# Sparse attention and a gated feed-forward layer on one core: 120 score columns in place of 128, sums of exponentials in SBUF, and the first operations in another written order

## The chip, the cores and the metric

The kernel runs on one core of one Trainium2 chip. The metric is the device time of one execution in microseconds; the median of the runs is compared. The engines are TensorE (PE, with its weight loads shown as PEld), VectorE (DVE), ScalarE (ACT), GpSimd (POOL) and SyncE (SP), which issues nearly all DMAs.

## The reference

```python
# q, k, v: 4 batches, 8 heads, 768 positions, 64 dims, float32
k_sum = k.reshape(B, H, 24, 32, D).max(axis=3)       # summaries of blocks of 32
v_sum = v.reshape(B, H, 24, 32, D).mean(axis=3)
scores_l = scale * q @ k^T, kept where abs(i - j) < 16, else -1e9
scores_s = scale * q @ k_sum^T + log(32)
a = softmax over the 768 + 24 columns (1e-9 added to the sum)
x = a @ concat(v, v_sum)          # as 3072 tokens of 512
out = ((x @ w_a) * (x @ w_b)) @ w_out                # d_ff 1536
```

## The kernel before, in words

**Attention.** A batch's 768 queries are 6 tiles of 128, so there are 24 tiles. Ten chunks `u` of 2, 2, 2, 2, 2, 2, 3, 3, 3 and 3 tiles go through the feed-forward layer together. A tile is worked on as two halves `e` of 64 queries. One half needs 96 keys of the window and the 24 summaries, 120 columns; before, a block of scores has 128 columns, the last 8 of them padding. `kT` holds the transposed keys in periods of `PER` = 160 columns per tile: 96 of the window, 24 summaries, 8 zeros, 32 further keys. `scores` issues 32 matmuls per tile (4 head pairs, 2 heads, 2 halves), which use a quarter of the array each.

In the first two chunks (`u < 2`, `masked`) the mask is added by PE: `masks` multiplies an identity `identr` with `maskr`, 512 columns at a time, into the PSUM banks `o0` to `o3`, and the scores are added on top. ACT's exponentials (L746, eight per tile) read the bank and write `s` to SBUF; `accum_out` writes the sum of each into column 0 of the very block in the bank. DVE adds 1e-9 (L756), takes the reciprocal (L767), makes a diagonal of it (L774), and PE turns and normalizes the exponentials with this diagonal (L795). In the later chunks DVE adds the mask (L724), takes the negative maximum (L732), ACT takes the exponentials with sums in the small SBUF tile `nml`, POOL multiplies with the reciprocal (L782), and DVE transposes 32 rows by 256 columns at a time (L827). `products` (L843) multiplies with the values `vw`; ACT and DVE split the result into two fp32r parts `x` (L862, L866).

**Queries, values and means of the later chunks.** `qin` is filled by 16 loads per tile and DVE transposes it into `qT` (L1049). `prep_values` lets POOL add blocks of values in `S` (L624), scale the mean into `vm` (L649), and SP store its eight rows of heads to `S`; two loads bring them from there into `vw`. All of these transfers go through L342 on SP's queue.

**Weights.** The raw weight blocks (`raw`, L374) are converted: ACT scales (L409), DVE makes three steps (L417, L424, L430), ACT casts the high part (L462), POOL makes the low part (L467, L473). PSUM banks `c0`, `c1` serve the conversion and later the scores.

**Feed-forward.** An item is one of 12 blocks of 128 of d_ff for one chunk: matmuls `up` (L1097), ACT copy (L1129), DVE product (L1132), ACT cast (L1134), DVE subtraction (L1137), matmuls `down` (L1174).

**Order.** Every operation is recorded in `Work` with a rank and an estimated time, and has a number. `emit` issues first what the lists in `ORDER` name, one list per engine and in that order; after its end an engine takes the ready operation of lowest rank. An engine executes its instructions in the order of issue. `SPIN` (L1263) is a list of matmuls without use, which fill PE at the start and are ranked in `ORDER` too, with the numbers from 2701.

Of the kernel before, what the change touches and what calls it, by code (L numbers as in the profile page):

```python
# [15 lines left out]
ALU = mybir.AluOpType  # L16
AX = mybir.AxisListType
LOG32 = 3.4657359027997265
NEG = -1.0e9
# [12 lines left out]
        922-924 931 929 930 873 936-938 945 943 944 952 950 1015  # L32
    """,
    "ACT": """
        2 10 6 18 14 22 56 76 194 61-63 70 71 64 68 69 81 198 83 84 89 88 91 90 82 112 205 208
# [8 lines left out]
        932 934 939 941 946 948 878-882 885 953 886  # L44
    """,
    "DVE": """
        3 7 19 15 11 23 195 59 60 196 80 79 65 197 66 72 73 199 67 200 201 92 85 74 86 93 87 94
        209 210 213 211 214 215 223-225 126 227 125 228 155 156 138 131 139 132 140 133 117 147
# [6 lines left out]
        377 479 373 656 480 658 481 483-485 663 382 665 496 378 670 497 381 498 672 500-502 384  # L55
        383 677 732 511 513 733 514 512 734 679 735 745 684 736 746 520 747 737 686 738 527 739
        748 749 691 530 539 537 750 693 541 535 531 532 711 540 534 751 533 536 538 752 758 759
        713 718 702 760 708 761 771 762 763 772 764 773 765 720 774-776 912 832 777 778 914 698
        836 919 872 921 834 837 835 850 926 928 843 725 933 864 935 858 860 857 865 866 862 868
        863 867 940 942 861 859 874 947 875 949 876 877 883 1014 954  # L60
    """,
    "POOL": """
        36-38 29 26 32 35 95 97 101 99 105 103 203 206 217 110 108 204 220 207 218 231 221 232
        234 235 248 249 262 263 276 277 290 291 304 305 334 335 348 349 397 398 411 412 425 426
        439 365 453 372 454 456 440 457 470 471 473 474 487 488 490 491 504 505 507 508 529 521
        528 782-785 788 789 753 790-792 766 740 779 793 800-803 1405 851 844 806 1406 807 808
        1407 809-811 1409-1412 884
    """,
    "SP": """
# [14 lines left out]
    ("h1", 512), ("h1", 128), ("h1", 64), ("h1", 64), ("h1", 64), ("h1", 128), ("h1",  # L84
    128), ("h1", 128), ("h1", 128), ("h1", 128), ("h1", 256), ("h1", 256), ("h1", 256),
    ("h1", 128), ("h1", 256)
# [76 lines left out]
def attention_moe(  # L163
# [10 lines left out]
    nc = tc.nc  # L174
# [47 lines left out]
    PER = 160  # L222
# [5 lines left out]
    for c in range(NP):  # L228
        nc.gpsimd.memset(kper[:, c, :, WIN + NS : WIN + 32], 0.0)
# [5 lines left out]
    for i in range(3):  # L235
        for e in range(2):
            es = slice(e * QT, (e + 1) * QT)

            for c0, n, w in ((0, 96, 0),) if e == 0 else ((0, 32, 0), (64, 64, 32)):
# [12 lines left out]
            nc.gpsimd.memset(mask[es, i, k0 : k0 + NS], LOG32)  # L252
            nc.gpsimd.memset(mask[es, i, k0 + NS : k0 + 32], NEG)
# [3 lines left out]
    sbuf = sb([P, 2, NP, P], "s")  # L257
    pbuf = sb([P, 2, NP, P], "pt")
# [276 lines left out]
    def first_keys():  # L535
        n = P // BLK
        for i in range(S // P):
# [10 lines left out]
            def put(bk=bk, c0=c0):  # L548
# [3 lines left out]
                    out=kT[:, :, c0 + P : c0 + PER + 16], in_=tr[:, :, WIN - 16 :]  # L552
# [16 lines left out]
    def prep_keys(b):  # L569
# [3 lines left out]
        for c in range(NP):  # L573
# [5 lines left out]
            for takes, o, i in (  # L579
                (0.7, kper[:, c, :, :WIN], groups[:, :, :WIN]),  # L580
                (0.26, kper[:, c, :, P:], groups[:, :, WIN:]),
# [9 lines left out]
            for takes, o, i in (  # L591
                (0.65, half[:, :, :6], kper[:, c, :, :WIN].rearrange(x16, x=16)),
                (0.26, half[:, :, 6:], kper[:, c, :, P:].rearrange(x16, x=16)),
# [65 lines left out]
    def load_values(b, t, vw, keys, rank):  # L659
# [3 lines left out]
        for i, (e, r0, lo, hi) in enumerate((  # L663
            (0, skip, row - 16 + skip, row + 80),
            (1, 0, row + 48, row + 80),
            (1, 64, row + 80, end),
# [6 lines left out]
    def scores(u, t, qT, qk, s, sk, banks, diag=None, lead=None):  # L673
# [7 lines left out]
        def masks():  # L681
            for h in range(2):
                for part in range(2):
                    nc.tensor.matmul(
                        bank[banks[h]].rearrange("p (c x) -> p c x", x=P), identr,
# [614 lines left out]
```

## Time and profile before

| | |
|---|---|
| median of 3 runs | 668.29 us (667.89 to 670.66) |
| profiled execution | 667.98 us |
| its span in the profile | 666.2 us |
| mean granted PE clock | 0.999 |
| PE busy | 652.4 us, 98% of the span |
| DVE, ACT, POOL busy | 419.3, 257.4, 190.6 us |

The span is what the profiler records between the first and the last instruction; the execution's own time is 1.78 us longer. The rows quoted below give a start or a group, then its length in microseconds, the engine, the line of the code, and what is written from what, without the numbers of the buffers. A bracket at the end of a row is the idle time just before it and what ended it.

### The profile page before, as it was taken

What the parts mean: (1) busy time and instruction counts of PE and PEld (TensorE: products, weight loads), DVE (VectorE), ACT (ScalarE), POOL (GpSimd) and SP (SyncE); (2) the same over time, 40 slices, a digit from 0 to 9 for tenths busy, and PEclk for the clock granted to TensorE, in tenths of its full rate; (3) what the DMA queues carried; (4) which work ended last, traced back from release to release, by engine and by line L of the source; (5) the groups of instructions that cost most, each with busy time, mean ns of one, the idle gap of its engine ahead of it and who ended that gap; (6) DMA issues with size and microseconds to landing.
All of it is one profiled execution on the core that took longest, in us unless ns stands there. A gap on an engine that the chain in (4) does not pass through costs nothing.

```text
span 666.2 us, 14017 instructions
## 1 busy us (share of the span) xinstructions
PE 652.4 (98%) x5442; PEld 610.7 (92%) x5442; DVE 419.3 (63%) x900; ACT 257.4 (39%) x791; POOL 190.6 (29%) x255
## 2 busy tenths in 40 slices
PE   8899999999999999999999999999999999999996
PEld 6689999999899999999999999999999999999996
DVE  3999999996677777567677755686662531122222
ACT  4996675523444432234334413333331411121111
POOL 6588989755344432011111100101110100000000
PEclk9999999999999999999999999999999999999999
DMA  9999747365343244412122331232000200010001
GB/s 219 270 272 274 262 116 176 64 139 125 94 87 94 69 94 98 78 32 71 30 41 50 77 58 32 41 86 41 17 10 1 70 1 0 1 48 1 0 1 48
DMA packets 156619, 54.78 MB, mean 82 GB/s; under 512 B 134008, under 2 KB 149624, under 8 KB 156552
## 3 DMA queue, kind: packets, MB, share of 16 engines
q1 hardware_dynamic: 156408, 53.75, 33.8%
q8 instruction: 42, 0.69, 0.5%
q14 instruction: 25, 0.20, 0.1%
q10 hardware_dynamic: 144, 0.13, 0.1%
HBM read 47.12 MB, written 6.29 MB: 80 GB/s over the span
## 4 chain that ended last, share of the span: by engine, by line
PE 74%; DVE 9%; SPq 7%; DMA 6%; issue 2%; ACT 2%; POOL 1%; DVEq 0%; POOLq 0%
PE h L1097 44%; PE o L1174 23%; SPq L342 6%; DMA raw<-in_moe_w_b_dram 3%; PE o L843 3%; PE c L697 2%; DMA raw<-in_moe_w_out_dram 2%; DVE c L424 1%; SPq L374 1%; DVE S L827 1%; DVE S L417 1%; DVE h L1132 1%; DVE S L430 1%; DVE space L430 1%; DVE pt L827 1%
## 5 line engine op out<-in xcount | busy, mean ns | idle before, releaser
L1097 PE MATMUL h<-x,w 128*128 128x256 f32 (+1 forms) x2488 | 396.0, 295 | 0.0
L1097 PEld LDWEIGHTS h<-x,w 128*128 128x128 f32 x2488 | 356.2, 191 | 4.7 <-issue 0.2
L1097 PE MATMUL h<-late,w 128*128 128x256 f32 (+1 forms) x380 | 114.1, 300 | 0.0
L1174 PE MATMUL o<-w,gh 128*128 128x512 f32 x426 | 107.2, 383 | 0.0
L827 DVE STREAM_TRANSPOSE pt<-s 32x256 f32<-32x256 f32 x228 | 99.4, 436 | 11.5 <-POOL s L782 5.7
L782 POOL TENSOR_TENSOR s<-s,nml 128x512 f32<-128x512 f32 x40 | 41.6, 1040 | 211.7 <-DVE nml L767 210.2
L1160 DVE TENSOR_TENSOR h<-h,g 128x384 f32<-128x384 f32 x47 | 26.6, 566 | 112.1 <-PE h L1097 109.9
L1174 PEld LDWEIGHTS o<-w,gh 128*128 128x128 f32 x426 | 76.6, 189 | 9.6 <-issue 1.5
L1162 ACT CAST gh<-h 128x384 fp32r<-128x384 f32 x47 | 22.5, 479 | 143.0 <-DVE h L1160 142.5
L746 ACT ACTIVATE s<-s,nml 128x128 f32<-128x128 f32 x160 | 62.3, 391 | 38.1 <-DVE nml L732 38.1
L1097 PEld LDWEIGHTS h<-late,w 128*128 128x128 f32 x380 | 72.3, 190 | 1.1
L1129 ACT COPY g<-h 128x256 f32<-128x256 f32 x72 | 26.7, 370 | 101.5 <-PE h L1097 101.2
L1174 PE MATMUL o<-w,gl 128*128 128x512 f32 x213 | 60.0, 381 | 0.0
L1174 PE MATMUL o<-w,x 128*128 128x512 f32 x225 | 56.2, 382 | 0.0
L1132 DVE TENSOR_TENSOR h<-h,g 128x256 f32<-128x256 f32 x72 | 30.7, 426 | 29.4 <-ACT g L1129 28.3
L624 POOL TENSOR_TENSOR S<-S 96x256 f32<-96x256 f32 (+3 forms) x58 | 33.1, 572 | 54.5 <-DMA S<-in_v_dram 51.9
L1174 PEld LDWEIGHTS o<-w,gl 128*128 128x128 f32 x213 | 39.8, 189 | 6.4 <-DVE gl L1137 0.6
L1174 PEld LDWEIGHTS o<-w,x 128*128 128x128 f32 x225 | 40.1, 190 | 5.5 <-issue 0.5
L724 DVE SCALAR_TENSOR_TENSOR s<-c,mask 128x512 f32<-128x512 f32 x40 | 27.2, 684 | 19.6 <-PE c L697 19.6
L1157 ACT COPY g<-h 128x384 f32<-128x384 f32 x48 | 23.0, 479 | 41.0 <-PE h L1097 40.9
L1165 DVE TENSOR_TENSOR gl<-h,gh 128x384 fp32r<-128x384 f32 x47 | 26.1, 555 | 17.9 <-ACT gh L1162 17.5
L467 POOL TENSOR_TENSOR space<-space,w 128x1024 f32<-128x1024 f32 (+1 forms) x14 | 26.7, 1914 | 12.0 <-ACT w L462 11.6
(130 smaller groups left out, 654.8 us busy)
## 6 DMA issues: line engine op xcount, KB each, us to landing
raw<-in_moe_w_a_dram SPq DMA_DIRECT2D x12, 512.0 KB
raw<-in_moe_w_b_dram SPq DMA_DIRECT2D x12, 512.0 KB
raw<-in_moe_w_out_dram SPq DMA_DIRECT2D x12, 512.0 KB
out_dram<-S SPq DMA_DIRECT2D x23, 256.0 KB
S<-in_v_dram SPq DMA_DIRECT2D x24, 192.0 KB
kin<-in_k_dram SPq DMA_DIRECT2D x38, 100.0 KB
vw<-in_v_dram SPq DMA_DIRECT2D x18, 192.0 KB
qin<-in_q_dram SPq DMA_DIRECT2D x192, 16.0 KB
```

Of the source, the lines that this page charges most:

```text
L342: lambda: nc.sync.dma_start(out=out, in_=in_), rate=rate,
L467: lambda ms=ms, f8=f8: nc.gpsimd.tensor_tensor(out=f8, in0=f8, in1=parted(0)[:, ms].bitcast(F32), op=ALU.subtract),
L624: lambda: nc.gpsimd.tensor_tensor(out=out, in0=i0, in1=i1, op=ALU.add),
L724: lambda h=h: nc.vector.scalar_tensor_tensor(out=s[h], in0=bank[banks[h]].rearrange("p (c x) -> p c x", x=P), scalar=0.125, in1=mask[:, ki ...
L746: lambda h=h, c=c, sums=sums: nc.scalar.activation(s[h][:, c, :], x[h][:, c, :], AF.Exp, bias=m[:, 0, h, c : c + 1], scale=1.0, accum_out= ...
L782: lambda h=h, r=r: nc.gpsimd.tensor_tensor(out=s[h], in0=s[h], in1=r[:, :, None].broadcast_to([P, NP, P]), op=ALU.mult,),
L827: lambda js=js, qs=qs, rs=rs: nc.vector.transpose(out=pv[js, rs, qs], in_=sv[qs, rs, js]),
L1097: nc.tensor.matmul(ps, w[:, c, part, :], inputs_of(u, xpart)[:, :, c].rearrange("p g (a b) -> p g b a", a=2), start=(i == 0), stop=(i == n ...
L1129: act(CHAIN, 0.38, [hk], [gk], lambda: nc.scalar.copy(out=g, in_=pa))
L1132: lambda: nc.vector.tensor_tensor(out=pa, in0=pb, in1=g, op=ALU.mult),
L1160: lambda: nc.vector.tensor_tensor(out=pb, in0=pb, in1=g, op=ALU.mult),
L1174: nc.tensor.matmul(bank[ok[j]], (gh if first else gl)[:, j * P : (j + 1) * P], w[:, :, part, :].rearrange("p (z a) n -> p z n a", a=2), st ...
```

## The change

The block of scores has `KN` = 120 columns, and `PER` is 152. All operations on scores, mask and exponentials take 120 (or 4 x 120 = 480) columns; the matmuls that turn them, and the products, contract over 120 rows. The memsets of the padding in `kT` and in the mask go; one memset of the padding of `s` comes. In the first two chunks the exponentials' sums go to `nml` in SBUF, and the addition of 1e-9 reads them there. The lists in `ORDER` are written anew and go further than before on DVE, ACT, POOL, SP and PE; `SPIN` has 16 matmuls of other widths in place of 15. The lines of the code shift by two to four.

```diff
-    PER = 160
+    PER = WIN + NS + 32
+    KN = WIN + NS
...
-    for c in range(NP):
-        nc.gpsimd.memset(kper[:, c, :, WIN + NS : WIN + 32], 0.0)
...
-            nc.gpsimd.memset(mask[es, i, k0 + NS : k0 + 32], NEG)
...
+    nc.gpsimd.memset(sbuf[:, :, :, KN:], 0.0)
...
-                        bank[banks[h]].rearrange("p (c x) -> p c x", x=P), identr,
-                        maskr[part][:, kind, None, :].broadcast_to([P, NP, P]),
+                        bank[banks[h]].rearrange("p (c x) -> p c x", x=P)[:, :, :KN], identr,
+                        maskr[part][:, kind, None, :KN].broadcast_to([P, NP, KN]),
...
-                            bank[banks[h]][es, c * P : (c + 1) * P], qT[hs, c, es],
-                            kT[hs, c, c0 : c0 + P],
+                            bank[banks[h]][es, c * P : c * P + KN], qT[hs, c, es],
+                            kT[hs, c, c0 : c0 + KN],
...
-            sums = x[h][:, :, 0] if masked else l
+            sums, r = l, x[h][:, :, 0] if masked else l
...
-                        out=r, in0=r, scalar1=1e-9, scalar2=None, op0=ALU.add
+                        out=r, in0=l, scalar1=1e-9, scalar2=None, op0=ALU.add
...
-                        bank[banks[h]][:, c * P : (c + 1) * P], s[h][:, c, :], d[:, h, c, :],
+                        bank[banks[h]][:KN, c * P : (c + 1) * P], s[h][:, c, :KN], d[:, h, c, :],
...
-                            ps[h * D : (h + 1) * D, c, es], vw[e][:, 2 * c + h, :],
-                            d[:, h, c, es], start=True, stop=True, tile_position=(0, h * D),
+                            ps[h * D : (h + 1) * D, c, es], vw[e][:KN, 2 * c + h, :],
+                            d[:KN, h, c, es], start=True, stop=True, tile_position=(0, h * D),
```

```diff
 SP, the first numbers of its list in ORDER
-        0 8 4 16 12 20 39 40 186 42 44 41 43 187 46 45 189 190 53 192 54 193 49 48 52 47 50 51
+        12 0 4 8 39 16 20 40 186 187 42 41 44 43 45 189 53 46 190 54 192 193 47 49 48 50-52 237
```

SP, the first loads of the program (`space` holds keys, queries and values in pieces, `raw` a weight block). Before:

```order
L342 DMA space_183<-in_k_dram 128x8x64 x3
L342 DMA space_184<-in_k_dram 128x8x64
L342 DMA space_183<-in_k_dram 128x8x64
L342 DMA space_184<-in_k_dram 128x8x64
L342 DMA space_184<-in_q_dram 128x8x64 x2
L374 DMA raw_208<-in_moe_w_a_dram 128x4x256
L342 DMA space_185<-in_v_dram 128x4x128 x4
L374 DMA raw_208<-in_moe_w_b_dram 128x4x256
```

and now:

```order
L344 DMA space_174<-in_k_dram 128x8x64 x4
L344 DMA space_175<-in_q_dram 128x8x64
L344 DMA space_175<-in_k_dram 128x8x64 x2
L344 DMA space_175<-in_q_dram 128x8x64
L376 DMA raw_199<-in_moe_w_a_dram 128x4x256
L376 DMA raw_199<-in_moe_w_b_dram 128x4x256
L344 DMA space_176<-in_v_dram 128x4x128 x4
```

One block of queries now stands ahead of the last two blocks of keys, and the second weight block ahead of the four blocks of values.

SP, the end of the `qin` loads of the tile whose scores run at 175.71 us in the profile, and the transfers of the value means around them. Before:

```order
L342 DMA qin<-in_q_dram 32x8x32 x2
L342 DMA S_181<-in_v_dram 96x512
L342 DMA out_dram<-S_182 128x512
L342 DMA S_182<-vm 24x64 x3
L342 DMA qin<-in_q_dram 32x8x32
L342 DMA S_182<-vm 24x64
L342 DMA qin<-in_q_dram 32x8x32
L342 DMA vw_165<-S_182 24x512
```

and now:

```order
L344 DMA qin<-in_q_dram 32x8x32 x4
L344 DMA S_173<-vm 24x64
L344 DMA qin<-in_q_dram 32x8x32
L344 DMA S_173<-vm 24x64
L344 DMA qin<-in_q_dram 32x8x32
L344 DMA S_173<-vm 24x64 x2
L344 DMA vw_156<-in_v_dram 80x8x64
L344 DMA S_172<-in_v_dram 96x512
L344 DMA vw_157<-in_v_dram 32x8x64
L344 DMA vw_156<-S_173 24x512
```

Two of the four stores of means that stood ahead of the last `qin` load stand behind it now, and the loads of the means into `vw` follow a little later.

PE, the matmuls from just ahead of these scores to the products that follow (`c_77`, `c_78` are the banks of the scores, `o_71` and `o_72` those of the feed-forward output). Before:

```order
L1174 MATMUL o_71<-w_969,x 128x512 x2
L1174 MATMUL o_72<-w_969,x 128x512 x2
L697 MATMUL c_77<-kT,qT 64x128 x2
L697 MATMUL c_78<-kT,qT 64x128 x2
...
L1174 MATMUL o_71<-w_969,x 128x512
L1174 MATMUL o_72<-w_969,x 128x512
L1174 MATMUL o_71<-w_1164,gh 128x512 x2
L1174 MATMUL o_72<-w_1164,gh 128x512 x2
L843 MATMUL o_74<-pt,vw_165 64x64 x2
```

and now:

```order
L1178 MATMUL o_71<-w_976,x 128x512
L1178 MATMUL o_72<-w_976,x 128x512
L699 MATMUL c_77<-kT,qT 64x120 x2
L699 MATMUL c_78<-kT,qT 64x120 x2
...
L1178 MATMUL o_71<-w_1146,gh 128x512 x2
L1178 MATMUL o_72<-w_1146,gh 128x512 x2
L1178 MATMUL o_71<-w_1146,gl 128x512
L1178 MATMUL o_72<-w_1146,gl 128x512
L847 MATMUL o_74<-pt,vw_156 64x64 x2
```

Two `down` matmuls moved from behind the scores to ahead of them, and two others from behind the products to ahead of them.

More of the change, by code (lines that the diff above doesn't have):

```diff
@@ L25 @@
     "PE": """
[6 rows of a table removed]
-        922-924 931 929 930 873 936-938 945 943 944 952 950 1015
+        2701 2702 13 2703 1 2704 5 2705 2706 55 9 2707 17 2708 2709 21 57 75 77 58 78 2710-2712
+        96 98 2713 100 2714 143 102 104 111 113 121 141 106 123 151 124 153 154 2715 2716 115
+        145 171 173 542 180 175 178 549 547 182 548 554-556 563 570 561 562 568 575 577 569 584
[5 rows of a table added]
     """,
     "ACT": """
-        2 10 6 18 14 22 56 76 194 61-63 70 71 64 68 69 81 198 83 84 89 88 91 90 82 112 205 208
[8 rows of a table removed]
-        932 934 939 941 946 948 878-882 885 953 886
[7 rows of a table added]
@@ L45 @@
+        499 671 489 676 678 503 506 522 683 523-526 516 517 685 515 518 519 690 692 710 712 701
+        717 719 707 911 696 913 918 920 845 848 846 838 839 925 840 841 927 723 842 847 849 932
+        934 939 941 946 948 881 887 953 885 955 878 879 886 888 889 880 882 960 962 870 967
     """,
     "DVE": """
-        3 7 19 15 11 23 195 59 60 196 80 79 65 197 66 72 73 199 67 200 201 92 85 74 86 93 87 94
-        209 210 213 211 214 215 223-225 126 227 125 228 155 156 138 131 139 132 140 133 117 147
[6 rows of a table removed]
@@ L55 @@
[L55 to L60, printed above, removed]
+        3 15 7 11 19 23 195 196 60 59 80 199 197 200 79 92-94 201 65 66 72 67 85 73 74 86 209 87
@@ L61 @@
+        210 211 213-215 126 125 223 224 155 156 138 225 139 131 227 132 140 133 117 228 147 229
[3 rows of a table added]
+        595 357 355 358 356 389-391 393 600 394 602 395 403 404 607 405 407 609 408 417 409 418
[7 rows of a table added]
+        866-868 860 858 859 861 876 874 877 875 947 1014 949 954 725 956 890 1049 883 898 899
+        903 895 904 897 902 961 963 871 896 905 901 900
     """,
     "POOL": """
-        36-38 29 26 32 35 95 97 101 99 105 103 203 206 217 110 108 204 220 207 218 231 221 232
-        234 235 248 249 262 263 276 277 290 291 304 305 334 335 348 349 397 398 411 412 425 426
@@ L65 @@
-        439 365 453 372 454 456 440 457 470 471 473 474 487 488 490 491 504 505 507 508 529 521
-        528 782-785 788 789 753 790-792 766 740 779 793 800-803 1405 851 844 806 1406 807 808
-        1407 809-811 1409-1412 884
+        36-38 29 26 32 35 97 95 101 99 103 105 206 203 108 110 207 204 220 217 218 231 221 232
+        234 235 248 249 262 263 276 277 290 291 304 305 334 335 348 349 397 398 411 412 372 425
+        365 426 439 440 453 454 456 457 470 471 473 474 487 488 490 491 529 504 505 507 528 521
@@ L68 @@
+        508 782-785 788 789 753 790 740 791 792 766 779 793 800-803 1405 844 1406 851 806 1407
+        807-811 1409-1412 1414 891 884 1415-1417 1419 1420
     """,
     "SP": """
[8 rows of a table removed]
+        12 0 4 8 39 16 20 40 186 187 42 41 44 43 45 189 53 46 190 54 192 193 47 49 48 50-52 237
[8 rows of a table added]
     """,
@@ L83 @@
 SPIN = [
-    ("h1", 512), ("h1", 128), ("h1", 64), ("h1", 64), ("h1", 64), ("h1", 128), ("h1",
-    128), ("h1", 128), ("h1", 128), ("h1", 128), ("h1", 256), ("h1", 256), ("h1", 256),
-    ("h1", 128), ("h1", 256)
+    ("h1", 512), ("h1", 128), ("h1", 64), ("h1", 64), ("h1", 256), ("h1", 256), ("h1",
+    64), ("h1", 128), ("h1", 128), ("h1", 256), ("h1", 256), ("h1", 256), ("h1", 256),
+    ("h1", 256), ("h1", 256), ("h1", 256)
 ]
@@ L237, in attention_moe @@
             es = slice(e * QT, (e + 1) * QT)
-            for c0, n, w in ((0, 96, 0),) if e == 0 else ((0, 32, 0), (64, 64, 32)):
+            for c0, n, w in ((0, 96, 0),) if e == 0 else ((0, 32, 0), (32 + NS, 64, 32)):
                 sl = mask[es, i, c0 : c0 + n]
@@ L551, in put @@
                 nc.scalar.copy(
-                    out=kT[:, :, c0 + P : c0 + PER + 16], in_=tr[:, :, WIN - 16 :]
+                    out=kT[:, :, c0 + KN : c0 + PER + 16], in_=tr[:, :, WIN - 16 :]
                 )
@@ L580, in prep_keys @@
                 (0.7, kper[:, c, :, :WIN], groups[:, :, :WIN]),
-                (0.26, kper[:, c, :, P:], groups[:, :, WIN:]),
+                (0.26, kper[:, c, :, KN:], groups[:, :, WIN:]),
                 (0.15, kT[:, c, KC - 32 :], kw[:, S:]),
@@ L592, in prep_keys @@
                 (0.65, half[:, :, :6], kper[:, c, :, :WIN].rearrange(x16, x=16)),
-                (0.26, half[:, :, 6:], kper[:, c, :, P:].rearrange(x16, x=16)),
+                (0.26, half[:, :, 6:], kper[:, c, :, KN:].rearrange(x16, x=16)),
                 (0.1, ks[:, c, NS - 1, None], kT[:, c, KC - 32 : KC - 16]),
@@ L665, in load_values @@
             (1, 0, row + 48, row + 80),
-            (1, 64, row + 80, end),
+            (1, 32 + NS, row + 80, end),
         )):
@@ L715, in scores @@
             lead[3]()
-        x = [bank[n].rearrange("p (c x) -> p c x", x=P) for n in banks] if masked else s
+        y = [bank[n].rearrange("p (c x) -> p c x", x=P)[:, :, :KN] for n in banks]
+        s = [t[:, :, :KN] for t in s]
+        x = y if masked else s
         xk = banks if masked else sk
@@ L724, in scores @@
                     lambda h=h: nc.vector.scalar_tensor_tensor(
-                        out=s[h], in0=bank[banks[h]].rearrange("p (c x) -> p c x", x=P),
-                        scalar=0.125, in1=mask[:, kind, None, :].broadcast_to([P, NP, P]),
+                        out=s[h], in0=y[h],
+                        scalar=0.125, in1=mask[:, kind, None, :KN].broadcast_to([P, NP, KN]),
                         op0=ALU.mult, op1=ALU.add,
@@ L751, in scores @@
             lk = [f"{mk}l{h}{c}" for c in range(NP)]
-            r = sums
             if masked:
@@ L755, in scores @@
                     rank, 0.15, [xk[h]], lk,
[L756 to L757 removed]
+                    lambda l=l, r=r: nc.vector.tensor_scalar(
+                        out=r, in0=l, scalar1=1e-9, scalar2=None, op0=ALU.add
                     ),
@@ L782, in scores @@
                     lambda h=h, r=r: nc.gpsimd.tensor_tensor(
-                        out=s[h], in0=s[h], in1=r[:, :, None].broadcast_to([P, NP, P]),
+                        out=s[h], in0=s[h], in1=r[:, :, None].broadcast_to([P, NP, KN]),
                         op=ALU.mult,
@@ L807, in transposes @@
                     lambda h=h: nc.scalar.copy(
-                        out=d[:, h], in_=bank[banks[h]].rearrange("p (c x) -> p c x", x=P)
+                        out=d[:KN, h],
+                        in_=bank[banks[h]].rearrange("p (c x) -> p c x", x=P)[:KN],
                     ),
@@ L991, in first_attention @@
         for e, r0 in ((0, WIN), (1, 32)):
-            rows = slice(r0, r0 + 32)
+            rows = slice(r0, r0 + NS)
             act(
```

1 line of the change is left out of this document (removed), and 57 rows, old and new, of the table ORDER.

## The prediction

> **What bounds the kernel now.** I read the page's head first, then a table of windows by stage, then TensorE's waits, and only then the chain around the two places where TensorE stands still.
>
> ```profile
> span 666.2 us, 14017 instructions
> PE 652.4 (98%) x5442; PEld 610.7 (92%) x5442; DVE 419.3 (63%) x900; ACT 257.4 (39%) x791; POOL 190.6 (29%) x255
> ```
>
> TensorE (PE) works 652.4 of 666.2 us, so two things alone can shorten the span: fewer microseconds of matmul, or part of the 13.8 us in which PE is idle. The windows say where these lie (the columns after the length are PE, PEld, DVE, ACT, POOL, then the granted clock, which is full everywhere).
>
> ```profile
> 0.00:20.00 20.00, 16.14 (x132) 11.76 (x132) 9.32 (x16) 10.00 (x33) 12.85 (x64) 1.00 1.08 236
> 20.00:40.00 20.00, 17.02 (x209) 14.07 (x209) 18.35 (x39) 19.11 (x64) 11.79 (x12) 1.00 1.03 265
> 40.00:60.00 20.00, 20.00 (x203) 19.02 (x202) 19.99 (x40) 16.81 (x34) 17.77 (x10) 1.00 1.13 288
> 80.00:145.00 65.00, 65.00 (x553) 61.12 (x552) 62.31 (x131) 37.32 (x92) 52.19 (x37) 1.00 0.54 127
> 170.00:180.00 10.00, 8.52 (x106) 7.25 (x105) 5.64 (x14) 5.28 (x22) 5.70 (x10) 1.00 0.30 78
> 180.00:640.00 460.00, 460.00 (x3725) 436.06 (x3724) 259.95 (x572) 143.96 (x487) 59.70 (x93) 1.00 0.20 45
> 640.00:666.20 26.20, 20.72 (x116) 19.27 (x114) 5.67 (x11) 4.37 (x10) 0.00 (x0) 0.97 0.09 31
> ```
>
> Idle PE: 3.86 and 2.98 us in the first 40, 1.48 between 170 and 180, 5.48 at the tail, none elsewhere. In the first 40 us PE is not the bound (its work there is partly filler); what counts is when the feed-forward part starts. From then on PE is a solid row: the end is the start of that row, plus its matmuls, plus the one stall, plus the tail, which the change leaves as it is.
>
> ```profile
> 39.70 2.92 PE L1097 MATMUL h<-x,w 128*128 128x256 f32 x24
> PE c L697 <- DVE qT L1049: 1.5, 1, 1.5
> ```
>
> So the row starts at 39.70, and the stall is one wait of scores for the transposed queries. The profiled execution took 667.98 us (1.78 around the span); the median of the runs shown is 668.29, 0.05% more, so I add up against 667.98. A difference under 0.5%, 3.3 us, is about what a measurement of this kernel cannot tell from none.
>
> **Term 1: the scores lose 8 of 128 columns.** In chunks 2 to 9 there are 640 score matmuls, 32 for each of 20 tiles.
>
> ```profile
> L697 PE MATMUL c<-kT,qT 64*64 64x128 f32 x640 | 22.3, 275 | 1.5 <-DVE qT L1049 1.5
> L843 PE MATMUL o<-pt,vw 128*64 128x64 f32 x608 | 22.2, 225 | 0.0
> 175.71 1.10 PE c L697 x32
> 178.31 1.08 PE o L843 x32
> 180.02 5.36 PE h L1097 x48
> 372.86 3.90 PE h L1097 x24
> ```
>
> The first two rows are groups by shape; the others are pieces of the chain. 256 columns of the feed-forward matmul take 5.36/48 = 0.112 us, 384 columns 3.90/24 = 0.1625: 0.40 ns per column. The scores run four at a time, one per quarter of the array; eight fours in 1.10 us are seven steps and one duration of 0.275, 0.118 a step, close to the 0.112 of a 256-column pass. I read a four as 128 f32 columns gone over twice. Then 8 columns are worth 16 x 0.40 = 6.4 ns a four, 0.051 us a tile, 1.0 us over 20 tiles. Bounds: 0 if weights or issue pace the fours, and for this speaks that the products (L843), with half the columns, take 1.08 us for 32; 1.10/16 x 20 = 1.4 if all of the time is columns. I take **-1.0**, because with the products the weights have 128 rows and the single matmul is 225 ns against 275, so it is the columns that the longer one shows.
>
> The Trainium skill, TensorE: Matmul & The Clock Gate, section "Back-to-back issue gap", says that in a stream of weight loads and matmuls the spacing is set by both and gives about 81 ns for 128 columns. By that rule the loads could hide the columns and this term would be 0, the third rival below; the product row agrees with it, the score row does not decide.
>
> The 16 mask matmuls go from 512 to 480 columns, all before the row starts at 39.70, where PE has idle time: 0. The matmuls that turn the normalized scores and the products contract over 120 rows instead of 128, with the same columns: 0, between -0.1 and 0.1 (the score matmul with 64 rows and the product with 128 take the same 1.1 us for 32).
>
> **Other engines' shorter operations, after 40 us.** The mask addition, the maximum (0.68 us each on DVE), the exponentials and POOL's multiplication shrink by up to 1/16. From 180 to 640 DVE works 260 of 460 us, and PE never waits: 0. If anything were later there, the feed-forward items ahead of each attention step cover it; without that cover the chain of a tile would be some 0.04 us shorter at the addition and at the maximum (0.68/16), 20 x 0.08 = 1.6 us over the tiles, a gain. From 40 to 145 DVE is full, but PE has no idle there either, so its few shortened operations can only add slack. Eight memsets go and one comes, on POOL at the start, where it works 12.85 of 20 us: 0.
>
> **Term 2: the stall at 174 us.** SP issues the 16 `qin` loads of a tile; the last lands at 174.76 and DVE's transpose and the scores follow.
>
> ```profile
> 169.25 2.30 SPq L342 DMA_DIRECT2D S<-vm  x3
> 171.59 0.52 SPq L342 DMA_DIRECT2D qin<-in_q_dram  x1
> 172.16 0.72 SPq L342 DMA_DIRECT2D S<-vm  x1
> 172.92 0.51 SPq L342 DMA_DIRECT2D qin<-in_q_dram  x1
> 172.92 1.84 DMA qin<-in_q_dram
> 174.94 0.71 DVE L1049 STREAM_TRANSPOSE qT<-qin 128x512 f32<-128x512 f32 x1 [1.74 <-DMA qin<-in_q_dram]
> 175.71 1.10 PE L697 MATMUL c<-kT,qT 64*64 64x128 f32 x32 [1.48 <-DVE qT L1049]
> 173.97 0.75 SPq L342 DMA_DIRECT2D vw<-S  x1
> 175.33 0.73 SPq L342 DMA_DIRECT2D vw<-S  x1
> ```
>
> Before, four stores of value means (`S<-vm`, 0.72 to 0.77 us each) stand between or just ahead of the last loads; in the changed order two do, and the last load stands eight places earlier on SP. Two stores fewer bring it 1.5 us forward; the places passed (0.45 to 0.75 us each) more still, unless a store waits for POOL. From the issue to the scores it takes 175.71 - 172.92 = 2.79 us, so queries ready at 174.2 or earlier. PE was ready at 174.23 and now has two down matmuls (0.43 us) ahead of the scores. The wait goes: -1.48. What is late next are the mean rows `vw<-S`: the two loads now follow the stores closely, and the second issue, at 175.33 before, would land at about 176.5 if all of SP moves 1 us forward and a load takes the 1.84 us of the one above; the products would reach PE at about 176.55. A new wait lies between 0 and 0.5. The whole term lies between -1.48 and 0 (the wait kept, or turned into one at the products); I take **-1.4**.
>
> **Term 3: the start.** Two chunks' exponentials sum into column 0 of the PSUM bank that the next one reads; now they sum into SBUF.
>
> ```profile
> 9.24 0.66 PE L492 MATMUL o<-ident,space 128*128 128x128 f32 x4 [0.28 <-DMA space<-in_k_dram]
> 10.52 0.63 PE L492 MATMUL c<-ident,space 128*128 128x128 f32 x4 [0.17 <-DMA space<-in_k_dram]
> 17.77 0.37 ACT L746 ACTIVATE s<-o,nml 128x128 f32<-128x128 f32 x1
> 18.09 0.37 ACT L746 ACTIVATE s<-o,nml 128x128 f32<-128x128 f32 x1
> 18.55 0.37 ACT L746 ACTIVATE s<-o,nml 128x128 f32<-128x128 f32 x1
> 157.34 0.39 ACT L746 ACTIVATE s<-s,nml 128x128 f32<-128x128 f32 x1
> 157.72 0.39 ACT L746 ACTIVATE s<-s,nml 128x128 f32<-128x128 f32 x1
> L732 DVE TENSOR_REDUCE nml<-o 128x4 f32<-128x512 f32 x8 | 5.2, 681 | 0.1
> DVE space L417 <- ACT c L409: 3.6, 2, 3.0
> 15.50:40.00 24.50, 20.75 (x250) 16.21 (x249) 22.69 (x46) 22.12 (x78) 14.22 (x15) 1.00 1.06 274
> ```
>
> The PSUM sums start 0.32 or 0.46 us after one another (0.40 on the mean of two), those with SBUF sums 0.385. The new ones read PSUM and sum into SBUF, which no row shows; between 0.32 and 0.385 is likely, so 32 exponentials give ACT 0.5 to 2.6 us. But DVE decides: from 15.5 to 40 it works 22.69 of 24.50 us, and the same operations stand ahead of the first `x` as before. Of these, eight maxima and nothing else get shorter: 8 x 0.68/16 = 0.34. What can move beyond this is DVE's idle, at most 1.5 us until 39.48. The second raw weight block is asked for four places earlier, which can close the 0.6 us of DVE's second wait for ACT; against this, the first scores now wait for a key block that stands behind a query block on SP (the two key blocks of the first rows are 1.28 us apart), though DVE has two weight operations of 0.69 to do meanwhile. So the first `x` comes 0.3 to 0.9 us earlier, at the ends 1.9 earlier or 0.9 later.
>
> Not all of it reaches the end, for one item has no slack:
>
> ```profile
> 53.27 2.39 POOL L467 TENSOR_TENSOR space<-space,w 128x1024 f32<-128x1024 f32 x1 [0.38 <-DMA raw<-in_moe_w_b_dram]
> 60.56 2.39 POOL L473 TENSOR_TENSOR w<-space 128x1024 fp32r<-128x1024 f32 x1
> 63.01 2.84 PE L1097 MATMUL h<-x,w 128*128 128x256 f32 x24
> ```
>
> POOL's chain of low parts runs without a gap from 53.27 to 62.95 and PE takes its result at 63.01. If the chain does not move forward as well, PE waits there and returns the gain. The chain depends on DVE, whose load ahead of it falls by the same 0.34. I take **-0.5**, between -1.9 and +0.9.
>
> The Trainium skill, ScalarE: Activation LUTs, section "Step-by-step: what each stage is for", holds that ScalarE writes PSUM sooner than SBUF, which speaks against moving the sums. The trace agrees only where no exponential waits for the bank (0.32 against 0.385); in this order half of them wait.
>
> **Sum:** 667.98 - 1.0 - 1.4 - 0.5 = **665.1 us**.
>
> **Rivals.**
> A. The start gains all of DVE's idle: 667.98 - 1.0 - 1.4 - 1.9 = 663.7. For it: ACT, 19.11 of 20 us busy, gets time back and raw weights come sooner. Against it: the low-part chain without slack.
> B. The stall turns into a wait for `vw<-S` at the products, or stays: 667.98 - 1.0 - 0.5 = 666.5. For it: the mean rows land within 0.1 us of their use by my estimate.
> C. Weights or issue pace the scores and columns bring nothing: 667.98 - 1.4 - 0.5 = 666.1. For it: the products' equal 1.08 us.
> D. Exponentials with SBUF sums are no shorter than 0.40 and come on the path: 32 x 0.02 = 0.6 more on ACT in place of the gain, start +0.1: 665.7.
> E. Slower: the changed order of the conversions lets the low-part chain slip by two of its links, 2 x 2.39 = 4.8 us, and PE waits for it at 63: 667.98 + 4.8 - 1.0 - 1.4 = 670.4. It decides for slower than before when the slip passes 2.4 us, about one link, and beyond 0.5% when it passes 5.7. For it: no slack at 62.95; against it: POOL's list there keeps the same sequence, and DVE's is one operation different.
>
> **How the numbers follow.** Chances: the sum 0.37 (its own range 664.3 to 665.9), A 0.22, B 0.16, C 0.12, D 0.05, E 0.08. Faster by over 0.5% means under 664.95: A's 0.22 and somewhat under half of the sum's case, 0.18, and 0.03 where B or C meet a good start: 0.43. Slower by over 0.5%, over 671.6: under half of E, 0.03. Within 0.5%: 0.54. The range, 663.4 to 667.3, leaves out E (0.08) and the lower part of A (0.07) and what B and C make together with a late start (0.05).
>
> **What the profile after would show.** Score groups of 32 in about 1.05 us in the chain; no wait of L699 for `qT` near 174, and none of the products for `vw`; exponentials of the first 40 us at an even spacing of 0.32 to 0.385; first feed-forward matmul near 39.2; the item at 63 not waiting for POOL. The prediction is wrong if that item or another between 45 and 100 us waits for POOL's chain, or if new one-time waits come up between 145 and 300, where the orders differ too and I found none to expect.

## The result, and the profile after

The changed kernel takes 663.18 us (median of 5 runs, 663.09 to 663.52) against 668.04 us before on the same chip: a ratio of 0.9921, 95% interval 0.9902 to 0.9940, 4.9 us less. The forecast was 2.9 us less, 665.1, and its range reached down to 663.4. Each profile is of one execution; where an experiment's runs scatter, the time of the execution that was profiled stands beside what is read from it.

The head of the page after, and the windows that answer to those of before:

```profile
span 661.4 us, 14028 instructions
PE 650.5 (98%) x5444; PEld 609.1 (92%) x5444; DVE 415.1 (63%) x900; ACT 254.4 (38%) x791; POOL 188.2 (28%) x246
...
0.00:20.00 20.00, 16.05 (x134) 12.02 (x134) 9.70 (x16) 9.66 (x30) 12.66 (x55) 1.00 1.09 241
20.00:40.00 20.00, 17.80 (x218) 14.82 (x218) 18.54 (x43) 19.18 (x69) 11.75 (x12) 1.00 1.06 264
170.00:180.00 10.00, 10.00 (x123) 8.90 (x123) 6.35 (x16) 4.94 (x22) 3.71 (x6) 1.00 0.51 132
180.00:640.00 460.00, 460.00 (x3718) 436.04 (x3717) 255.40 (x569) 144.00 (x488) 57.89 (x93) 1.00 0.21 46
640.00:661.40 21.40, 16.77 (x92) 15.24 (x90) 4.56 (x9) 3.42 (x8) 0.00 (x0) 0.99 0.11 38
```

The window at 170 has no idle PE any more, and the last one has 4.63 us of it instead of 5.48. The timeline of PE after, at the start of the feed-forward row, at the scores that had waited, and at the last matmuls:

```profile
38.70 2.94 PE L1101 MATMUL h<-x,w 128*128 128x256 f32 x24
172.76 1.05 PE L699 MATMUL c<-kT,qT 64*64 64x120 f32 x32
175.23 1.15 PE L847 MATMUL o<-pt,vw 120*64 120x64 f32 x32
654.64 2.21 PE L1178 MATMUL o<-w,x 128*128 128x512 f32 x9
```

The row starts 1.00 us earlier (39.70 before), and neither these scores nor these products wait. For the account I took from the trace, for each matmul from the row's first on, the time until the next one starts, and added it up by line (so a wait ahead of a group is booked on the line of the matmul before it):

| part of the span | before | after | difference | forecast |
|---|---|---|---|---|
| up to the first feed-forward matmul | 39.70 | 38.70 | -1.00 | -0.5 |
| scores, 640 matmuls | 20.88 | 19.62 | -1.26 | -1.0 |
| products, 704 matmuls | 24.23 | 23.80 | -0.43 | 0 |
| down matmuls, the stall included | 191.54 | 190.26 | -1.28 | -1.4 |
| up and normalizing matmuls | 384.00 | 384.09 | +0.09 | 0 |
| last matmul's start to the end | 5.81 | 4.92 | -0.89 | 0 |
| span | 666.2 | 661.4 | -4.8 | -2.9 |

### The profile page after: what moved, and what is told of

The parts are those of the page before. It is cut to its first block, busy times and chain, and to the rows that moved or that the text cites. A ratio compares the mean times of both kernels' runs of the same rounds, so it can differ in the third digit from the quotient of the medians.

```text
span 661.4 us, 14028 instructions
## 1 busy us (share of the span) xinstructions
PE 650.5 (98%) x5444; PEld 609.1 (92%) x5444; DVE 415.1 (63%) x900; ACT 254.4 (38%) x791; POOL 188.2 (28%) x246
## 4 chain that ended last, share of the span: by engine, by line
PE 91%; DMA 4%; DVE 2%; SPq 1%; issue 0%; POOL 0%; ACT 0%; DVEq 0%; ACTq 0%; POOLq 0%
PE h L1101 55%; PE o L1178 27%; PE o L847 3%; PE c L699 3%; DMA raw<-in_moe_w_out_dram 1%; SPq L344 1%; PE o L798 1%; DMA raw<-in_moe_w_b_dram 1%; DMA raw<-in_moe_w_a_dram 1%; DMA qin<-in_q_dram 1%; DVE nml L736 1%; DVE space L419 0%; POOL space L469 0%; PE c L847 0%; DVE c L426 0%
## 5 line engine op out<-in xcount | busy, mean ns | idle before, releaser
L785 POOL TENSOR_TENSOR s<-s,nml 128x480 f32<-128x480 f32 x40 | 39.5, 989 | 217.1 <-DVE nml L770 215.3
L750 ACT ACTIVATE s<-s,nml 128x120 f32<-128x120 f32 x160 | 61.3, 386 | 39.6 <-DVE nml L736 39.6
L728 DVE SCALAR_TENSOR_TENSOR s<-c,mask 128x480 f32<-128x480 f32 x40 | 25.8, 652 | 15.6 <-PE c L699 15.3
L750 ACT ACTIVATION_READ_ACCUMULATOR s<-s,nml 128x1 f32 x160 | 30.3, 189 | 0.0
```

The source lines that it names most:

```text
L728: lambda h=h: nc.vector.scalar_tensor_tensor(out=s[h], in0=y[h], scalar=0.125, in1=mask[:, kind, None, :KN].broadcast_to([P, NP, KN]), op0 ...
L750: lambda h=h, c=c, sums=sums: nc.scalar.activation(s[h][:, c, :], x[h][:, c, :], AF.Exp, bias=m[:, 0, h, c : c + 1], scale=1.0, accum_out= ...
L785: lambda h=h, r=r: nc.gpsimd.tensor_tensor(out=s[h], in0=s[h], in1=r[:, :, None].broadcast_to([P, NP, KN]), op=ALU.mult,),
```

## The experiments

**Columns and order apart.** Two kernels each make half of the change.

```diff
 (cols_oldorder: the changed kernel)
-ORDER = {...}; SPIN = [...]   # of the changed kernel
+ORDER = {...}; SPIN = [...]   # of the kernel before
```

> The changed kernel with the lists ORDER and SPIN of before: the 120 columns, the shorter products and the sums in SBUF alone. Theory 1 (the gain is a sum of separate parts, the narrower matmuls one of them): the scores take 1.3 us less and the products 0.4 us less on TensorE between the first feed-forward matmul and the end, that matmul starts 0.3 to 0.6 us earlier than at 39.70, the 1.5 us wait for qT near 174 stays: 665.6 to 666.4. Theory 2 (the order makes all of the gain, columns are hidden by weight loads): 667.6 to 668.0, and the 640 score matmuls keep their spacing.

```diff
 (neworder_128: the kernel before)
-ORDER = {...}; SPIN = [...]   # of the kernel before
+ORDER = {...}; SPIN = [...]   # of the changed kernel
```

> The kernel before with the changed lists ORDER and SPIN: the order alone, 128 columns, sums in PSUM. Theory 1: the wait near 174 is 0.2 us or less, the first feed-forward matmul is 0.4 to 0.7 us earlier than at 39.70, the stretch after the last matmul is 0.9 us shorter if the order is what moved it: 665.0 to 666.2. Theory 2: 663.2 to 663.6, as the changed kernel.

Columns alone: 666.87 us (665.22 to 671.6, 12 runs) against 668.09, ratio 0.9984 (0.9968 to 1.0); the profiled execution took 665.96, its span is 664.3. Order alone: 664.85 us (664.56 to 665.39), ratio 0.9953 (0.9941 to 0.9965), span 663.0. So neither makes the whole of the gain: theory 2 falls. Theory 1 has the parts, but both its ranges are missed (666.87 is above 666.4, 664.85 just under 665.0). By the medians the halves give 1.2 and 3.2 us. The spans of the two profiles are 1.9 and 3.2 us shorter than before; the first is of an execution 0.9 us under its median. PE's timeline of the columns alone, then of the order alone:

```profile
38.64 2.59 PE L1098 MATMUL h<-x,w 128*128 128x256 f32 x21
174.68 1.05 PE L696 MATMUL c<-kT,qT 64*64 64x120 f32 x32 [1.77 <-DVE qT L1050]
```

```profile
38.72 2.50 PE L1100 MATMUL h<-x,w 128*128 128x256 f32 x20
173.86 1.10 PE L700 MATMUL c<-kT,qT 64*64 64x128 f32 x32
```

Each alone brings the row's start to 38.6 or 38.7, and so do both together: the 1.0 us at the start is there once. So the two spans, without counting it twice, make 4.1 us of the whole change's 4.8; of the other 0.7, 0.3 is a longer stall in the columns' profile and 0.4 slower `up` matmuls in the order's (382.61 us against 382.23 in the changed kernel). The stall stays with the columns alone (1.77) and is gone with the order alone. The scores take 19.88 us with the columns alone, 20.69 with the order alone: columns give 1.00 in the old order and 1.07 in the new one. The products' 0.43 is the order's (23.79 with 128 rows): before, one group of 32 at 43.4 took 1.39 us and one at 141.6 took 1.20, where all others take 1.08, and a score group at 73.7 took 1.20 instead of 1.034. Of the 0.4 us that theory 1 gave to the products with the columns alone, 0.06 came (24.17). Such small waits lie inside a group, where the waits' list did not name them.

**The rows of the products.**

```diff
-                            ps[h * D : (h + 1) * D, c, es], vw[e][:KN, 2 * c + h, :],
-                            d[:KN, h, c, es], ...
+                            ps[h * D : (h + 1) * D, c, es], vw[e][:kn, 2 * c + h, :],
+                            d[:kn, h, c, es], ...     # kn = 128 from chunk 2 on
```

> The changed kernel with the products of chunks 2 to 9 over 128 rows as before (rows 120 to 127 are zero on both sides). Theory 1 (the 120 rows save TensorE time, 0.43 us over 704 matmuls): 663.5 to 663.7. Rival (the contraction length costs nothing, the 0.4 us is another effect at the same place, the narrower scores ahead of them): 663.1 to 663.3.

663.26 us (663.0 to 664.16), ratio to before 0.9930 (0.9918 to 0.9942), beside 0.9921 of the changed kernel: no difference that can be told. In its profile (of its slowest execution, 664.16 us) one group of 32 products, at 176.14, took 1.30 us from its first start to the next matmul's; every other takes 1.08, as with 120 rows. The rival holds; contracting over 120 rows instead of 128 is worth nothing here.

**How the scores are paced.** Two kernels leave out columns of the scores.

```diff
-        masked = u < FILL
+        masked = u < FILL
+        kn = KN if masked else 96      # 64 in scores_64
...
-                            bank[banks[h]][es, c * P : c * P + KN], qT[hs, c, es],
-                            kT[hs, c, c0 : c0 + KN],
+                            bank[banks[h]][es, c * P : c * P + kn], qT[hs, c, es],
+                            kT[hs, c, c0 : c0 + kn],
```

> The changed kernel with score matmuls of 96 columns in chunks 2 to 9 (the summaries are left out there; all else still works on 120 columns). Theory (columns pace the fours): 24 columns are worth three times the 1.05 us that 8 columns gave on the 640 score matmuls, 3.2 us: 659.8 to 660.3, and the scores take 16.5 us of TensorE. Rival (a floor of weight loads or issue lies just under 120 columns): 662.0 to 663.2.

> The changed kernel with score matmuls of 64 columns in chunks 2 to 9 (a third of the window and the summaries are left out). Theory: if columns pace the fours all the way down, 56 columns are worth 7.35 us: 655.6 to 656.2, scores 12.3 us. Rival (the floor that the products show, with 64 columns at 0.034 us a matmul, holds for scores too, or one a little under it): 16 to 21 us of scores, 659.5 to 663.

660.71 us (660.14 to 661.54) and 658.15 us (656.92 to 659.21). The pieces of the chain that hold one tile's 32 scores, each from its kernel's own chain: before (128 columns), the changed kernel (120), 96, 64.

```profile
480.58 1.03 PE c L697 x32
```

```profile
172.83 0.98 PE c L699 x32
```

```profile
481.86 0.82 PE c L700 x32
```

```profile
478.17 0.62 PE c L700 x32
```

From row to row 8, 24 and 32 columns go, and 0.05, 0.16 and 0.20 us: 6.3 to 6.7 ns a column for the 32 matmuls at each step, down to 64 columns, and the 640 scores take 19.6, 16.4 and 12.5 us. There is no floor in this stretch, and the theory holds for the scores. Both times are longer than it gave (660.71 against at most 660.3, 658.15 against at most 656.2): in their profiles, of executions of 661.07 and 656.92 us, PE waits at places where it does not in the changed kernel, 0.36 and 0.22 us with 96 columns, 0.27 and 0.47 with 64. One of these waits, with 96 columns, is that of the products near 175 us for the means:

```profile
175.70 1.04 PE L848 MATMUL o<-pt,vw 120*64 120x64 f32 x28 [0.22 <-DMA vw<-S]
```

The products' 1.08 us for 64 columns is no sign of a floor either. The starts of the single matmuls in the traces show why. Scores start in fours, 7 ns apart; the next four starts 0.109, 0.103, 0.083 and 0.058 us after it with 128, 120, 96 and 64 columns. Products start in pairs, and the next pair starts 0.058 us after it, as a four of scores with the same 64 columns does. The equal times of 32 products and 32 scores come from 16 pairs beside 8 fours. The rule of the Trainium skill that I had set beside this term (TensorE: Matmul & The Clock Gate, "Back-to-back issue gap", some 81 ns for 128 columns) does not describe these fours: with 128 columns a score matmul follows the one before after 32 ns in the mean (1.034 us for 32).

**Where the sums go.** Once in the changed kernel, once in the kernel before.

```diff
 (sums_psum: the changed kernel)
-            sums, r = l, x[h][:, :, 0] if masked else l
+            sums = x[h][:, :, 0] if masked else l
+            r = sums
```

> The changed kernel with the exponentials' sums of the first two chunks in column 0 of the PSUM bank as before. Theory 1 (the exponentials in the first 40 us are 0.40 us apart again and the start waits for them): first feed-forward matmul 0.4 to 1.0 us later than at 38.70, 663.6 to 664.2. Rival (VectorE decides the start, the sums' place is hidden): 38.7, 663.1 to 663.3.

```diff
 (before_sums: the kernel before)
-            sums = x[h][:, :, 0] if masked else l
+            sums, r = l, x[h][:, :, 0] if masked else l
```

> The kernel before with one change: the exponentials' sums of the first two chunks go to SBUF; 128 columns and the old lists stay. Theory (in the old order VectorE waits 0.3 and 0.5 us for exponentials that wait for each other's bank): both waits go, the first feed-forward matmul starts 0.6 to 0.8 us earlier, near 39.0, and the time is 667.2 to 667.5. Rival (the earlier start with 120 columns came from VectorE's shorter maxima, 0.3 us, and from loads): start at 39.6 to 39.8, 667.9 to 668.1.

In the changed kernel the place is worth nothing: 663.17 us (662.95 to 663.44), start at 38.55. The traces show where it goes: with the sums in PSUM DVE waits 0.47 us for an exponential, but its wait for ACT's weight block, four microseconds later, is 0.48 shorter. DVE's timeline with the sums in PSUM, then of the changed kernel:

```profile
23.79 0.17 DVE L760 TENSOR_SCALAR o<-o 128x4 f32<-128x4 f32 x1 [0.47 <-ACT space L751]
27.86 0.69 DVE L419 TENSOR_SCALAR space<-c 128x512 int32<-128x512 int32 x1 [0.42 <-ACT c L411]
```

```profile
27.98 0.69 DVE L419 TENSOR_SCALAR space<-c 128x512 int32<-128x512 int32 x1 [0.90 <-ACT c L411]
```

In the old order no such wait follows DVE's longest one for an exponential, at 36.72 us, just ahead of the first `x`:

```profile
36.72 0.17 DVE L756 TENSOR_SCALAR o<-o 128x4 f32<-128x4 f32 x1 [0.52 <-ACT s L746]
```

With the sums in SBUF this wait is gone, as the theory had it, so are 0.25 us between the two additions L756 at 23.70, and the row of the kernel before starts 0.82 us earlier; but the time is 667.83 us (666.68 to 668.74) against 668.07, ratio 0.9990 (0.9977 to 1.0003). The interval leaves room for all of the 0.82 and for none of it. PE's timeline of the profiled execution (668.55 us, 0.7 above the median) shows waits behind the start:

```profile
38.88 2.37 PE L1096 MATMUL h<-x,w 128*128 128x256 f32 x19
48.07 1.15 PE L842 MATMUL o<-space,space 128*64 128x64 f32 x32 [0.31 <-ACT space L806]
58.41 0.70 PE L1173 MATMUL o<-w,gl 128*128 128x512 f32 x2 [0.18 <-DVE gl L1136]
```

From the row's start to the last matmul it takes 621.9 us where the kernel before takes 620.6: in this execution it gives back more than what it won at the start, between 45 and 65 us, with waits at 48, 58 and 62 us, two of which the rows name. One profile does not show that the sums' place is the cause. The kernel with ten memsets below has the code of the kernel before up to there, and in its profile, too, PE waits at 48.99 (0.45 us) and the row's first 240 matmuls take 25.79 us instead of 25.10; here they take 26.22. So whether a start won alone reaches the end is open.

The exponentials of the changed kernel, the first of them (ACT's timeline), follow one another evenly:

```profile
18.15 0.35 ACT L750 ACTIVATE s<-o,nml 128x120 f32<-128x120 f32 x1
18.49 0.36 ACT L750 ACTIVATE space<-o,nml 128x120 f32<-128x120 f32 x1
18.82 0.36 ACT L750 ACTIVATE space<-o,nml 128x120 f32<-128x120 f32 x1
19.16 0.37 ACT L750 ACTIVATE space<-o,nml 128x120 f32<-128x120 f32 x1
```

0.34 us apart, between the 0.32 and 0.46 of the PSUM sums. What the Trainium skill says of PSUM as ScalarE's faster destination (ScalarE: Activation LUTs, "Step-by-step: what each stage is for") is no reason here to leave the sums there: in the rows, sums in PSUM come 0.32 us apart only where no exponential waits for the bank, and 0.40 in the mean.

**The tail.** DVE's records before show 1090 instructions, after 1100 (those that the page does not count as busy included). A block of code of 8 KB is loaded when DVE nears its 1087th.

```diff
+        if u == 6 and f < 10:
+            dve(n, 0.07, ["g0"], ["tiny"], lambda: nc.vector.memset(tiny, 0.0))
```

> The kernel before with ten one-column memsets on VectorE, spread over chunk 6, where it works half of the time. In the records VectorE's eighth block of code is loaded as it nears its 1087th instruction: 3.3 us after the last matmul before, in the middle of the last output transfer, and 4.6 us ahead of the last matmul in the changed kernel, which has ten VectorE instructions more. Theory (this load slows the last output transfer): with ten more instructions it moves ahead of the last matmul, the stretch from the last matmul's start to the end falls from 5.8 to 4.9 us, 667.1 to 667.3. Rival (the tail is shorter for another reason, or by chance): 5.8 us and 668.0.

667.07 us (666.35 to 669.86, 10 runs) against 668.07: ratio 0.9985 (0.9971 to 0.9999). DMA of the last 6.2 us, first before, then with the ten memsets (mean throughput in 40 slices, packets, queues):

```profile
GB/s 0 0 0 0 0 0 0 0 0 0 277 370 304 410 383 317 377 383 390 397 330 350 331 370 86 13 7 7 13 13 0 0 0 0 0 0 0 0 0 0
DMA packets 577, 0.79 MB, mean 128 GB/s; under 512 B 64, under 2 KB 320, under 8 KB 576
...
q14 instruction: 1, 0.01, 0.3%
```

```profile
GB/s 0 0 0 0 0 0 0 0 0 0 0 0 0 0 0 0 282 376 322 389 376 336 349 396 383 376 363 376 296 369 168 0 0 0 0 0 0 0 0 0
DMA packets 576, 0.79 MB, mean 129 GB/s; under 512 B 64, under 2 KB 320, under 8 KB 576
```

Before, one packet of the instruction queue lies among the last output packets, and the transfer ends in a dribble of 7 to 13 GB/s over five slices of 0.155 us; with ten instructions more that packet comes 4.3 us ahead of the last matmul's start, and the transfer ends sharply. From the last matmul's start to the end it takes 4.91 us, as in the changed kernel (4.92), instead of 5.81. The theory holds: the 0.9 us is where DVE's code happens to be loaded. The other profiles agree: of all fourteen kernels here, the four in which this packet comes after the last matmul's start need 5.79 to 5.84 us from there to the end, and the ten in which it comes before need 4.91 to 4.95. How one packet holds up the transfer for so long is not shown. The span of the memsets' profile, 668.1 (an execution of 669.86 us, the slowest of the ten), holds longer waits elsewhere (2.1 us for `qT`), so only its tail is read.

**ScalarE's code at the last item.**

```diff
+        if u == 6 and f < 6:
+            act(n, 0.07, ["g0"], ["tiny"], lambda: nc.scalar.copy(out=tiny, in_=ident[:, :1]))
```

> The changed kernel with six one-column copies on ScalarE, spread over chunk 6. In the changed kernel ScalarE starts its copy of the last item's first half 0.34 us after the semaphore that released it, in three profiles of three with this number of ScalarE instructions, and 0.06 us after it in those with two fewer; TensorE then waits 0.48 us instead of 0.19 us for the last item. Theory (ScalarE crosses from one block of code to the next at that instruction): with six more it crosses earlier, the copy follows at 0.06 us, the wait is 0.19 us, 662.8 to 663.0. Rival (the order of the last items makes the wait): 663.1 to 663.3.

663.05 us (662.79 to 663.33), beside 663.18 of the changed kernel: too little to tell apart by time. The rows of ACT's timeline, first the changed kernel, then with six copies more:

```profile
652.99 0.49 ACT L1161 COPY g<-h 128x384 f32<-128x384 f32 x1 [1.13 <-PE h L1101]
```

```profile
652.69 0.48 ACT L1163 COPY g<-h 128x384 f32<-128x384 f32 x1 [0.86 <-PE h L1102]
```

The idle time ahead of the copy is 0.27 us shorter, and the down matmuls fall from 190.26 to 189.93 us. So a delay that depends on how many instructions ScalarE has executed stood on the path of the last item. That it is the crossing between two blocks of code is argued, not shown; for it speaks that an 8 KB load of code comes after 960 of ScalarE's records in both traces, at 653.64 us in the changed kernel, 0.65 after the start of that copy, and at 640.00 with six copies more.

**The stall at 174 us.** First SP's list alone, put into the kernel before:

```diff
 (before_sp: the kernel before; PE, DVE, ACT, POOL and SPIN as they were)
-    "SP": """..."""   # of the kernel before
+    "SP": """..."""   # of the changed kernel
```

> The kernel before with SP's changed list alone; the other engines keep their old lists. Theory (the stall near 174 comes from the stores of means on SP ahead of the last query load): the gap ahead of those scores falls from 1.5 to 0.3 us or less, and the earlier second weight block moves the first feed-forward matmul by up to 0.5 us: 666.2 to 666.9. Rival (it took TensorE's new list as well, with two matmuls moved ahead of the scores): a wait of 0.5 to 1.0 us stays, 667.0 to 667.5.

A miss for both: 675.22 us (673.56 to 676.89), ratio 1.0100 (1.0071 to 1.0130). No scores wait for `qT` near 174 any more, but the row starts at 42.91, and PE's longest wait is another:

```profile
PE o L1175 <- ACT x L1135: 2.9, 1, 2.9
```

Here one engine's list in the others' old order is worse than none. Therefore the two other runs move one load in the changed kernel, `1004` in SP's list:

```diff
-1003 814 1004 813 815 852 1413 853 855 856
+1003 814 813 815 1004 852 1413 853 855 856      # qin_back2
+1003 814 813 815 852 1413 853 855 1004 856      # qin_back6
```

> The changed kernel with one load moved on SP: the last qin load of the tile whose scores run at 172.76 stands behind the two stores of means it had been put ahead of. In the changed kernel its transposed queries are ready at 170.97, 1.8 us before TensorE needs them. Theory (the stall of before was this load's place on SP, and the change won more than the stall had): 1.5 us later is still in time, no wait near 173, 663.1 to 663.4. Rival (the two stores are the whole difference, as the prediction had it): a wait of 1 us or more, 664.0 to 664.7.

> The changed kernel with that load moved behind four further transfers as well, to just ahead of the second load of the means, where SP would issue it at about 172.8, as it did at 172.92 before. Theory: the scores wait for it again, until about 172.8 + 2.8 = 175.6, some 2.8 us, and the time is 665.3 to 666.2. Rival (TensorE's two matmuls moved ahead of the scores, or the queries' other loads, took the stall): a wait under 1 us, 663.2 to 664.0.

Two places: 664.8 us (663.09 to 666.11), ratio 0.9950 (0.9929 to 0.9972). The median lies by the rival's range, the profile speaks for the theory: it was taken of the fastest execution, 663.09 us, no scores wait near 173, and the row takes 617.75 us as in the changed kernel (617.77). But in that execution the load was hardly late, as SP's issue of it shows, first in the changed kernel, then two places back:

```profile
168.24 0.52 SPq L344 DMA_DIRECT2D qin<-in_q_dram  x1
```

```profile
168.54 0.52 SPq L344 DMA_DIRECT2D qin<-in_q_dram  x1
```

It comes 0.3 us later and not 1.5. So this run decides nothing, and what the slower executions waited for is not known. Six places: 667.45 us (665.4 to 671.89), above the theory's 666.2; in the profiled execution of 665.40 us, again the fastest, the wait is back, in another form. SP's issue of the load, then PE and DVE of that kernel:

```profile
171.56 0.51 SPq L344 DMA_DIRECT2D qin<-in_q_dram  x1
...
174.49 0.70 PE L1178 MATMUL o<-w,x 128*128 128x512 f32 x2 [1.55 <-DVE x L1141]
175.12 1.05 PE L699 MATMUL c<-kT,qT 64*64 64x120 f32 x32
...
173.41 0.71 DVE L1053 STREAM_TRANSPOSE qT<-qin 128x512 f32<-128x512 f32 x1 [2.79 <-DMA qin<-in_q_dram]
174.05 0.39 DVE L1141 TENSOR_TENSOR x<-h,x 128x256 fp32r<-128x256 f32 x1
```

DVE waits 2.79 us for the load with the transpose at the head of its queue, and the subtraction L1141 stands behind it; PE's two down matmuls need that subtraction and wait 1.55 us, ahead of the scores. So the load's place on SP can make the stall: 3.3 us later than in the changed kernel, it is back. I had expected 2.8 us at the scores: the load was issued 1.2 us earlier than I had reckoned, and the wait reaches PE through DVE's queue. In the changed kernel the transposed queries are ready 1.8 us ahead of their use.

## Why the prediction was wrong, point by point

**Term 1, the scores: right, and so was its reason.** 0.051 us a tile forecast, 0.053 measured (1.034 to 0.981 for 32). From 128 to 64 columns the step of a four shrinks by 0.8 ns a column, twice the 0.40 of a feed-forward column, as "gone over twice" has it. The bound of 0 was too wary: the equal time of the products that spoke for it came from two side by side instead of four. Rival C falls.

**Term 2, the stall: right in size** (-1.48 for the wait, no new one at the products), too small in its cause: the last load is issued at 168.24 instead of 172.92, 4.7 us earlier, where two stores gave 1.5. The rows were there to show it, since I counted eight places and then used two. That the size came out all the same is luck. Rival B did not occur in the changed kernel's profile, but it was near: scores 24 columns shorter bring its wait for `vw<-S` back (0.22 us, above). Its working had a slip: 175.33 - 1 + 1.84 is 176.17 and not 176.5, which left 0.4 us of margin and not 0.1.

**Term 3, the start: mis-sized**, -0.5 forecast, -1.00 measured. The caution after the sum of DVE's work took little off the 0.3 to 0.9 that stood there; the step that failed is that sum. "The same operations stand ahead of the first `x`" counted 0.34 for the maxima and, of DVE's idle, 0.6 for the second weight block. It left out that DVE itself waited for the exponentials, 0.52 us at 36.72 and 0.25 earlier: the sums alone are worth 0.82 in the old order. In the changed kernel they are worth nothing, and the order alone gives 0.98; which of its moves does so is open. The start also varies between executions: in the seven profiles of kernels with the changed kernel's operations up to there it lies between 38.43 and 39.06, in the two with those of before at 39.53 and 39.70. The idle of DVE was 1.8 us by the row's own numbers (24.50 - 22.69), not 1.5. POOL's operation that had ended at 62.95 ends at 62.44 now (its timeline row follows), and PE waits for none of the chain, so nothing was given back here.

```profile
60.05 2.39 POOL L475 TENSOR_TENSOR w<-space 128x1024 fp32r<-128x1024 f32 x1
```

Why the gain stayed is open. In the profile of the sums alone it was given back between 45 and 65 us, but one profile shows too little for that, as said above.

Rival A came nearest in time, 663.7 us. That is luck: it had 1.9 us at the start, which gave 1.0, and nothing for the tail and the products.

**The tail: the step that failed most.** "Plus the tail, which the change leaves as it is" put 0 where the runs show -0.89 us. No operation there changes; what changed is the count of DVE's instructions ahead of it, and with it the place where its code is loaded. Nothing in the views I had quoted showed this; the packets of the instruction queue in the last window would have.

**The small waits inside groups**, 0.6 us (products 0.43, one score group 0.17), had no term. "None elsewhere" was read from busy time, and a product's record is 0.22 us long where the next pair starts 0.058 us later, so records can still cover a wait. They were in the trace of before; two rows of PE's timeline there, each of 32 products:

```profile
43.45 1.46 PE L843 MATMUL o<-pt,vw 128*64 128x64 f32 x32
...
178.24 1.15 PE L843 MATMUL o<-pt,vw 128*64 128x64 f32 x32
```

The score group's 0.17 us brought nothing in the end. Before, its second half waited inside the group for DVE's L430; in the changed kernel another wait of the same group, for `qT`, stands ahead of its first matmul. Before, then after:

```profile
73.74 1.27 PE L697 MATMUL c<-kT,qT 64*64 64x128 f32 x32
```

```profile
74.04 1.05 PE L699 MATMUL c<-kT,qT 64*64 64x120 f32 x32 [0.16 <-DVE qT L1053]
```

**Rivals D and E** did not occur: exponentials 0.34 apart, no slip of the low-part chain.

Added up: the mis-sized start 0.5, the tail 0.9 and the small waits 0.6 are 2.0 us too little gain, and the line with the stall's term takes back 0.1 (it holds 0.3 us of ScalarE's delay at the last item and the 0.16 at 74.04).

## What to carry to other kernels

In this kernel, whose bound engine is 98% busy, the change of order was worth a sum of small one-time waits. So list every idle stretch of that engine, the tail included, and compare groups of the same shape with one another: a group of 32 that takes 1.39 us beside 1.08 hides a wait that no list names. Read also the waits of the engine that sets the start: a wait of 0.5 us in DVE's list was the larger part of what the sums won there. Before two small matmuls are compared by their times, see from their starts how many run side by side. And look where a moved load is issued in the very execution that was profiled: an edit of the list does not say by how much it came later.

## What the runs showed of the hardware

An 8 KB block of an engine's code, loaded after the last matmul's start, went with an end 0.9 us later (5.79 to 5.84 us against 4.91 to 4.95, fourteen profiles), and ten memsets of one column, far ahead, removed it. Four score matmuls on the quarters of the array are paced by their columns from 128 down to 64, at 6.3 to 6.7 ns a column for 32 matmuls; with 64 columns a four of them steps as fast as a pair of products on all rows, 0.058 us.
